# Where the even chunks of w_gate lie in SBUF: half of their rows moved 64 bytes past a multiple of 128

## The chip, the cores and the metric

The kernel runs on one core of a Trainium2 chip. The metric is device time in microseconds of one execution; the kernel before took 1170.16 us (median of three runs, 1168.32 to 1172.19). About 0.3% is what a measurement of this kernel can tell from no change.

## The reference

The program computes block-causal attention over 8 batches of 8 heads (576 positions, 64 dimensions a head) and feeds the result, as 4608 tokens of 512 features, through a gated feed-forward layer with 1536 hidden features.

```python
scores = scale * np.matmul(q, k.transpose(0, 1, 3, 2))      # masked by blocks of 64
attn = softmax(scores); x = attn @ v                        # as [4608, 512]
g = x @ w_gate                                              # [512, 1536]
silu = g * (1.0 / (1.0 + np.exp(-g)))
val = x @ w_val                                             # [512, 1536]
return (silu * val @ w_out).astype(np.float32)              # [1536, 512]
```

The three weights come as 64-bit floats, so each element is two 32-bit words for the kernel.

## The kernel before, in words

[...]

**Feed-forward tiles.** The 4608 tokens go in 18 tiles of 256. x of a tile lies in four pairs of SBUF tiles `xhl` (128 features d x 256 tokens, high and low). The 1536 hidden features go in 12 chunks of 128, and two chunks make a pair: `feed_forward` works on chunks i and i+1 together. For each pair, `up(i, 0, ...)` makes the gate (w_gate) and `up(i, 1, ...)` the value (w_val), each into one PSUM tile `gv` with the chunk i in its first 256 columns and the chunk i+1 in its second. Each chunk takes NDC = 4 rows of features d = 0..3, and three matmuls a row: 12 matmuls of 128x128 weights by 256 columns of x. So a pair is 12 matmuls with an even chunk of w_gate, 12 with an odd one, and 24 with w_val. In all there are 18 x 6 pairs, and 18 x 6 x 12 = 1296 matmuls on the even chunks. ScalarE (tanh) and VectorE then make the gated product, split it into `hhl`, and TensorE makes the down product of an earlier pair with w_out's tiles `wo`.

In tiles 0 to 3 (below FINE) each row of an up product is a task by itself, so that three matmuls can stand alone among other work. From tile 4 on, the 12 matmuls of a chunk, and the gate and value of a pair, follow each other.

**Weights in SBUF.** `weight(i, kind)` loads a chunk of a weight once, turns its 64-bit words into a float, and keeps a high part (ScalarE, L1016) and a low part (VectorE, L1019) in resident tiles. `w_at(which, x, i)` gives the place: w_val in `v_all0` and `v_all1` (x = 0 high, 1 low), the odd chunks of w_gate in `g_odd0` and `g_odd1`, the even ones in `g_even0` and `g_even1`. Each tile holds four rows d a chunk, [128 partitions, 4, columns]. Six chunks of w_out wait for a while in such places, too (AWAY), two of them in places of even chunks (c = 10 and c = 8); they are stored from there to `wo_d` in DRAM (L1038) and read there by the down products of tiles 0 and 1.

A small tile `gap` of 16 floats (64 bytes) stands between `v_all1` and `g_even0`. In the built program the tiles start at these bytes of each partition:

| tile | before | past a multiple of 128 |
|---|---|---|
| g_odd0, g_odd1 | 1,984, 14,272 | 64 |
| v_all0, v_all1 | 26,560, 51,136 | 64 |
| g_even0, g_even1 | 75,776, 88,064 | 0 |
| xhl (all), hhl, wo, parts, qk | 119,296 and on for xhl | 0 |

Every row of 128 weights has 512 bytes, and rows and chunks follow at multiples of 512 bytes, so a tile's remainder is that of each of its rows.

**Order.** `in_order` plans all tasks with a table of costs and writes out one order for each engine; nothing in it depends on addresses. Attention work of the batches (scores at L480, L607 and L691, products with v at L858) stands among the feed-forward products on TensorE until about 950 us.

Of the kernel before, what the change touches and what calls it, by code (L numbers as in the profile page):

```python
# [8 lines left out]
F32R = mybir.dt.float32r  # L9
# [9 lines left out]
def kernel(  # L19
# [17 lines left out]
    nc = tc.nc  # L37
# [3 lines left out]
    P = 128  # L41
# [5 lines left out]
    NDC = DM // P  # L47
    NFC = DFF // P
# [49 lines left out]
    const = ctx.enter_context(tc.tile_pool(name="const", bufs=1))  # L98
# [54 lines left out]
    def add(engine, cost, rank, fn, after=(), bufs=(), port=False, mode="", stage=""):  # L153


        t = Task(engine, cost, rank, fn, after, bufs, port, mode)
        for a in after:
            if a is not None:
                a.next.append(t)
                t.waits += 1  # L160
        for u in bufs:
            u.left += 1
        t.n, t.stage = len(tasks), stage
        tasks.append(t)
        return t


    def act_us(n, psum=False, more=0.0):
        return (0.05 if psum else 0.093) + n * 0.000833 + more

    def dve_us(n, one=False):
        return 0.07 + n * (0.00052 if one else 0.00104)

    def up_us(n):
        return n * 0.1134 + (0.012 if n < 3 * NDC else 0.0)
# [8 lines left out]
    def dma(rank, size, fn, after=(), bufs=(), n=1, engine="SP", packet=1024, late=0.0):  # L184

        t = add(engine, 0.5 * n, rank, fn, after, bufs)
        t.moves = size / packet * (9.5 + 0.0405 * packet) / 16e3
        t.late = 1.1 + late
        return t
# [15 lines left out]
    half_w, whole_w = [P, NDC, DFF // 2], [P, NDC, DFF]  # L205
    g_odd = [const.tile(half_w, F32R, name=f"g_odd{x}") for x in range(2)]
    v_all = [const.tile(whole_w, F32R, name=f"v_all{x}") for x in range(2)]
    const.tile([P, 16], F32, name="gap")
    g_even = [const.tile(half_w, F32R, name=f"g_even{x}") for x in range(2)]

    def w_at(which, x, i):

        if which:
            return v_all[x][:, :, i * P : (i + 1) * P]
        return (g_odd if i % 2 else g_even)[x][:, :, i // 2 * P : (i // 2 + 1) * P]

# [98 lines left out]
    for i in range(7):  # L317
        n = 2**i
# [620 lines left out]
    def words(ap):  # L939
        return ap.bitcast(I32) if wide else ap  # L940
# [11 lines left out]
    def weight(i, kind):  # L952

        R = PIECES[i][kind]
        raw = Buf("wo", "raw")
        away = AWAY.get(i) if kind == 2 else None
        wo = Buf("wo", "out") if kind == 2 and not away else None
        fs = slice(i * P, (i + 1) * P)

        parts = 1 if wo else NDC

        def part(j):
            if wo:  # L970
                return wo[0][:, j : j + 1]
            which, c = away or (kind, i)
            return w_at(which, j, c)

        def load():
            view = raw[0].rearrange("p (n m) -> p n m", n=NDC if kind < 2 else 1)
            if kind < 2:
                fs = slice(i * P * (1 + wide), (i + 1) * P * (1 + wide))
                src = words((w_gate, w_val)[kind])[:, fs].rearrange("(c p) f -> p c f", p=P)
            else:  # L980
                src = words(w_out)[i * P : (i + 1) * P, :].rearrange("p (n m) -> p n m", n=1)
            nc.sync.dma_start(out=view, in_=src)

        t = chain["w"] = dma(AHEAD.get((i, kind), R), 5e5, load, [chain["w"]], [raw], packet=1024 if kind < 2 else 4096)
        bufs = [raw, wo] if wo else [raw]

        def words_of(j):
            w = raw[0].rearrange("p (n t) -> p n t", t=1 + wide)[:, :, j]
            return w.rearrange("p (n m) -> p n m", n=parts)

        y = Buf("ob", "signs") if wide else None


        def signs():
            w = words_of(1).bitcast(F32)
            to = y[0].rearrange("p (n m) t -> p n m t", n=parts)[:, :, :, 1]
            nc.scalar.mul(to, w, 2.0**-60)  # L997

        def scaled():
            w = words_of(1).bitcast(F32)  # L1000
            nc.scalar.mul(w, w, 2.0**-112)


        def fraction():
            s = y[0].rearrange("p m t -> p (m t)").bitcast(I32).rearrange("p (n m) -> p n m", n=parts)
            nc.vector.scalar_tensor_tensor(
                words_of(0), words_of(0), 29, s, ALU.logical_shift_right, ALU.bitwise_or
            )

        def exponent():  # L1010
            nc.vector.scalar_tensor_tensor(
                words_of(0), words_of(1), 3, words_of(0), ALU.logical_shift_left, ALU.bitwise_or
            )

        def high():
            nc.scalar.copy(part(0), words_of(0).bitcast(F32))  # L1016

        def low():
            nc.vector.tensor_tensor(  # L1019
                part(1), words_of(0).bitcast(F32), part(0).bitcast(F32), ALU.subtract  # L1020
            )

        if wide:
            t = add("ACT", act_us(DM, more=0.13), R, signs, [t], [raw, y])
            f = add("DVE", dve_us(DM), R, fraction, [t], [raw, y], True)
            t = add("ACT", act_us(DM, more=0.06), R, scaled, [t], [raw])
            t = add("DVE", dve_us(DM), R, exponent, [t, f], [raw], True)
        t = w_high[i, kind] = add("ACT", act_us(DM, more=0.04), R, high, [t], bufs)
        t = add("DVE", dve_us(DM), R, low, [t], bufs, True)
        if kind == 2:  # L1030
            w_kept[i] = t, wo, part

            def store():
                if wo:
                    nc.sync.dma_start(out=wo_d[i], in_=wo[0].bitcast(F32))
                    return
                for j in range(2):
                    nc.sync.dma_start(  # L1038
                        out=wo_d[i][:, j].rearrange("p (n m) -> p n m", n=parts), in_=part(j).bitcast(F32)
                    )  # L1040

            t = dma(R, 5e5, store, [t], [wo] if wo else [], 2 if away else 1, packet=512 if away else 4096)
            if away:
                before_place.append((t, away))
        w_done[i, kind] = t
# [58 lines left out]
    def feed_forward(j, t0, w, xs):  # L1104
# [16 lines left out]
        def rank(i):  # L1121
            return (10.0 + (t0 + w * i / NFC) / S) if j > 1 else SIDE[j] + w * i / NFC / S

        def up(i, which, prev):

            ps = Buf("gv")
            ts = up_done[0]
            for y in range(2):

                for ds in [range(NDC)] if j >= FINE else [[d] for d in range(NDC)]:  # L1130

                    def products(ds=ds, y=y):
                        hi, lo = (w_at(which, k, i + y) for k in range(2))
                        o = ps[0][:, y * w : (y + 1) * w]
                        for d in ds:
                            xhi, xlo = (xs[d][1][k] for k in range(2))
                            first, last = d == 0, d == NDC - 1
                            nc.tensor.matmul(o, lhsT=hi[:, d], rhs=xhi[:, 0:w], start=first, stop=False)  # L1138
                            nc.tensor.matmul(o, lhsT=hi[:, d], rhs=xlo[:, 0:w], start=False, stop=False)  # L1139
                            nc.tensor.matmul(o, lhsT=lo[:, d], rhs=xhi[:, 0:w], start=False, stop=last)  # L1140

                    ts = add(
                        "PE",
                        up_us(3 * len(ds)),
                        rank(i),
                        products,
                        [ts, *(xs[d][0] for d in ds), w_done[i + y, which]],
                        [ps, *(xs[d][1] for d in ds)],
                        stage="up",
                    )  # L1150
                    ts.prev = prev
                    prev = ts if j >= FINE else None
            chain["up"] = up_done[0] = ts
            return ps, ts

        for i in range(0, NFC, 2):
# [11 lines left out]
            n = 2 * w  # L1168
# [29 lines left out]
            for y in range(2):  # L1198
                away = AWAY.get(i + y)
                if j == 0 or j == 1 and i + y < BOTH:  # L1200
                    wl, wo, w_part = w_kept[i + y]
                else:
                    wo, away = Buf("wo", "out"), None
# [103 lines left out]
    for i in range(NFC):  # L1307
        for kind in range(3):
            weight(i, kind)
# [173 lines left out]
```

## Time and profile before

| | |
|---|---|
| median of three runs | 1170.16 us |
| the profiled execution's own time | 1170.16 us |
| its span | 1168.3 us |
| TensorE busy (matmul) | 1154.0 us, 8788 instructions |
| VectorE, ScalarE, GpSimd busy | 743.8, 620.8, 317.2 us |
| idle time of TensorE that a wait explains, longest group | 2.2 us (a gate product behind VectorE's L1175) |

Busy time counts a matmul from its start to its modelled end, and matmuls overlap: 256 columns last some 280 ns and follow each other at less than half of that. The pace is therefore read from the distance of starts in the timeline, whose rows give start and duration in us. In the rows on stretches, the first numbers are the stretch and its length, then follow the busy time and the count of each engine, the granted clock of TensorE, the share of busy DMA and GB/s; with a tile named, they count that tile's matmuls on TensorE alone. In the rows of one line, three numbers are the shortest, median and longest duration in ns.

### The profile page before, as it was taken

The numbers are of one execution on the slowest core, as the hardware profiler recorded it, in microseconds if no ns is written. First come the engines' busy times: TensorE is split into PE (matmuls) and PEld (weight loads), VectorE is DVE, ScalarE is ACT, GpSimd is POOL, SyncE is SP. The second block draws the span as 40 slices with busy tenths as digits, with TensorE's granted clock in tenths as the row PEclk, the third lists the DMA queues.
The fourth block names the chain that finished last, engine by engine and source line by source line (L and its number), as shares of the span: only waits on it lengthen the run. The fifth ranks groups of instructions, "written<-read, shape, count | busy, mean of one in ns | idle before, by whom it ended". The sixth has DMA issues, their size and how long they took to land.

```text
span 1168.3 us, 22385 instructions
## 1 busy us (share of the span) xinstructions
PE 1154.0 (99%) x8788; PEld 1038.1 (89%) x8788; DVE 743.8 (64%) x1230; ACT 620.8 (53%) x1114; POOL 317.2 (27%) x139
## 2 busy tenths in 40 slices
PE   8999999999999999999999999999999999999998
PEld 7767888888898989899898989989898989999997
DVE  6998888768696649577474758647584753323222
ACT  6998866755665556473555638365564622212111
POOL 3122201163524422515232331524233430000000
PEclk9999999999999999999999999999999999999999
DMA  7858757675567447465647546556574335444342
GB/s 199 231 149 228 217 171 223 179 213 157 153 179 206 134 133 197 156 169 165 179 127 216 153 161 159 173 142 179 155 210 155 129 125 182 157 151 139 141 170 101
DMA packets 263786, 197.44 MB, mean 169 GB/s; under 512 B 190528, under 2 KB 228176, under 8 KB 263680
## 3 DMA queue, kind: packets, MB, share of 16 engines
q1 hardware_dynamic: 262704, 195.29, 57.5%
q8 instruction: 69, 1.13, 0.4%
q10 hardware_dynamic: 976, 0.72, 0.2%
q14 instruction: 37, 0.30, 0.1%
HBM read 171.57 MB, written 24.38 MB: 168 GB/s over the span
## 4 chain that ended last, share of the span: by engine, by line
PE 90%; ACT 5%; DVE 2%; DMA 1%; issue 0%; SPq 0%; POOL 0%; DVEq 0%; POOLq 0%; ACTq 0%
PE gv L1138 17%; PE gv L1140 16%; PE gv L1139 16%; PE at L858 8%; PE po L1230 8%; PE po L1231 7%; PE po L1232 7%; PE at L607 6%; PE at L480 1%; PE at L1230 1%; PE at L1231 1%; PE at L1232 1%; DMA wo<-in_moe_w_out_dram 1%; PE at L691 1%; ACT ob L997 1%; ACT sc L498 1%
## 5 line engine op out<-in xcount | busy, mean ns | idle before, releaser
L752 POOL PARTITION_ALL_REDUCE mx<-mx x80 | 139.8, 1799 | 414.4 <-DVE mx L748 118.2
L1138 PE MATMUL gv<-xhl,v_all 128*128 128x256 f32 x864 | 240.9, 279 | 1.4 <-DVE t L1180 1.3
L1140 PE MATMUL gv<-xhl,v_all 128*128 128x256 f32 x864 | 239.1, 277 | 0.0
L1139 PE MATMUL gv<-xhl,v_all 128*128 128x256 f32 x864 | 239.0, 277 | 0.0
L909 POOL PARTITION_ALL_REDUCE mx<-mx x48 | 174.8, 3693 | 223.7 <-DVE mx L748 186.7
L1175 DVE SCALAR_TENSOR_TENSOR t<-t,gv 128x512 f32<-128x512 f32 x108 | 74.0, 685 | 185.2 <-ACT t L1172 184.8
L1138 PEld LDWEIGHTS gv<-xhl,v_all 128*128 128x128 f32 x864 | 162.1, 188 | 3.7 <-DVE t L1180 2.0
L1139 PEld LDWEIGHTS gv<-xhl,v_all 128*128 128x128 f32 x864 | 162.2, 188 | 0.5
L1140 PEld LDWEIGHTS gv<-xhl,v_all 128*128 128x128 f32 x864 | 162.2, 188 | 0.0
L1185 ACT CAST hhl<-t 128x512 fp32r<-128x512 f32 x108 | 67.0, 621 | 174.8 <-PE po L1231 104.6
L1230 PE MATMUL po<-wo,hhl 128*128 128x512 f32 x372 | 147.7, 397 | 0.0
L1231 PE MATMUL po<-wo,hhl 128*128 128x512 f32 x372 | 145.5, 391 | 0.0
L1232 PE MATMUL po<-wo,hhl 128*128 128x512 f32 x372 | 145.1, 390 | 0.0
L1188 DVE TENSOR_TENSOR hhl<-t,hhl 128x512 fp32r<-128x512 f32 x108 | 84.2, 782 | 83.5 <-ACT hhl L1185 83.1
L1172 ACT ACTIVATE t<-gv 128x512 f32<-128x512 f32 x108 | 64.6, 598 | 129.2 <-PE gv L1140 127.2
L776 DVE TENSOR_TENSOR sc<-sc,mx 128x640 f32<-128x640 f32 (+6 forms) x168 | 121.8, 775 | 15.4 <-POOL mx L752 15.3
L1138 PE MATMUL gv<-xhl,g_even 128*128 128x256 f32 x432 | 124.1, 287 | 2.3 <-DVE t L1175 2.2
L1140 PE MATMUL gv<-xhl,g_even 128*128 128x256 f32 x432 | 122.1, 283 | 0.0
L1139 PE MATMUL gv<-xhl,g_even 128*128 128x256 f32 x432 | 122.1, 283 | 0.0
L1138 PE MATMUL gv<-xhl,g_odd 128*128 128x256 f32 x432 | 121.3, 281 | 0.0
L1140 PE MATMUL gv<-xhl,g_odd 128*128 128x256 f32 x432 | 119.4, 276 | 0.0
L1139 PE MATMUL gv<-xhl,g_odd 128*128 128x256 f32 x432 | 119.4, 276 | 0.0
(176 smaller groups left out, 2402.0 us busy)
## 6 DMA issues: line engine op xcount, KB each, us to landing
wo<-wo_d SPq DMA_DIRECT2D x200, 512.0 KB
out_dram<-ob SPq DMA_DIRECT2D x35, 256.0 KB
v<-in_v_dram SPq DMA_DIRECT2D x64, 128.0 KB
xt<-x_d SPq DMA_DIRECT2D x64, 128.0 KB
rt<-r_d SPq DMA_DIRECT2D x128, 64.0 KB
qk<-in_q_dram SPq DMA_DIRECT2D x104, 72.0 KB
qk<-in_k_dram SPq DMA_DIRECT2D x104, 72.0 KB
x_d<-xu SPq DMA_DIRECT2D x24, 288.0 KB
```

Of the source, the lines that this page charges most:

```text
L752: nc.gpsimd.partition_all_reduce(m, m, channels=P, reduce_op=bass_isa.ReduceOp.max)
L776: nc.vector.tensor_tensor(piece(c), scores_of(c), m, ALU.subtract)
L858: nc.tensor.matmul(ps[0][own(x), 1 - i if sums else i, q0 - s0 : s1 - s0], lhsT=ones if sums else vt[0][:, 2 * lane + c, own(x)], rhs=sc[0 ...
L909: nc.gpsimd.partition_all_reduce(m, m, channels=P, reduce_op=bass_isa.ReduceOp.add)
L1138: nc.tensor.matmul(o, lhsT=hi[:, d], rhs=xhi[:, 0:w], start=first, stop=False)
L1139: nc.tensor.matmul(o, lhsT=hi[:, d], rhs=xlo[:, 0:w], start=False, stop=False)
L1140: nc.tensor.matmul(o, lhsT=lo[:, d], rhs=xhi[:, 0:w], start=False, stop=last)
L1175: nc.vector.scalar_tensor_tensor(t[0][:, 0:n], t[0][:, 0:n], 1.0, pg[0][:, 0:n], ALU.add, ALU.mult)
L1188: nc.vector.tensor_tensor(hh[1][:, 0:n], t[0][:, 0:n], hh[0][:, 0:n].bitcast(F32), ALU.subtract)
L1230: nc.tensor.matmul(po, lhsT=hi, rhs=whi, start=i + y == 0, stop=False)
L1231: nc.tensor.matmul(po, lhsT=hi, rhs=wlo, start=False, stop=False)
L1232: nc.tensor.matmul(po, lhsT=lo, rhs=whi, start=False, stop=i + y == NFC - 1)
```

## The change

`g_even0` and `g_even1` become one tile `g_even` with two halves. The first half holds rows d = 0, 1 of every even chunk, high and low, the second half rows d = 2, 3. Each half is `apart` = 12 x 2 x 128 + 16 floats long, 12,352 bytes, which is 96 x 128 + 64; so the first half starts where `g_even0` did (75,776, a multiple of 128) and the second at 88,128, 64 bytes past one. `w_at` now returns a view [128, 2, 256] for an even chunk, and the new function `rows_of_w` finds row d in a view of either kind. `parts`, by which the conversion and the stores cut a chunk, becomes 2 for an even chunk instead of 4. The tile is 128 bytes longer than the two before, so all tiles behind it move up by 128 bytes (xhl from 119,296 to 119,424) and keep their remainder.

The order of instructions on every engine, their counts and their waits are the same in both programs. What differs, other than addresses, is the shape of some accesses: eight copies on ScalarE, eight subtractions on VectorE, four stores to `wo_d` and 18 down matmuls reach an even chunk's place as 2 x 256 instead of 4 x 128.

```diff
     const.tile([P, 16], F32, name="gap")
-    g_even = [const.tile(half_w, F32R, name=f"g_even{x}") for x in range(2)]
+    apart = NFC * NDC // 2 * P + 16
+    g_even = const.tile([P, 2 * apart], F32R, name="g_even")
...
         if which:
             return v_all[x][:, :, i * P : (i + 1) * P]
-        return (g_odd if i % 2 else g_even)[x][:, :, i // 2 * P : (i // 2 + 1) * P]
+        if i % 2:
+            return g_odd[x][:, :, i // 2 * P : (i // 2 + 1) * P]
+        o = (i + x) * NDC // 2 * P
+        return g_even.rearrange("p (h m) -> p h m", h=2)[:, :, o : o + NDC // 2 * P]
+
+    def rows_of_w(w, d):
+
+        n = NDC // w.shape[1]
+        return w[:, d // n, d % n * P : (d % n + 1) * P]
...
-        parts = 1 if wo else NDC
-
         def part(j):
...
+        parts = 1 if wo else part(0).shape[1]
...
-                            nc.tensor.matmul(o, lhsT=hi[:, d], rhs=xhi[:, 0:w], start=first, stop=False)
-                            nc.tensor.matmul(o, lhsT=hi[:, d], rhs=xlo[:, 0:w], start=False, stop=False)
-                            nc.tensor.matmul(o, lhsT=lo[:, d], rhs=xhi[:, 0:w], start=False, stop=last)
+                            nc.tensor.matmul(o, lhsT=rows_of_w(hi, d), rhs=xhi[:, 0:w], start=first, stop=False)
+                            nc.tensor.matmul(o, lhsT=rows_of_w(hi, d), rhs=xlo[:, 0:w], start=False, stop=False)
+                            nc.tensor.matmul(o, lhsT=rows_of_w(lo, d), rhs=xhi[:, 0:w], start=False, stop=last)
```

## The prediction

> **What bounds the kernel now.** I read the page's first two parts, then the stretches, then the timeline of TensorE.
>
> ```profile
> span 1168.3 us, 22385 instructions
> PE 1154.0 (99%) x8788; PEld 1038.1 (89%) x8788; DVE 743.8 (64%) x1230; ACT 620.8 (53%) x1114; POOL 317.2 (27%) x139
> PEclk9999999999999999999999999999999999999999
> PE 90%; ACT 5%; DVE 2%; DMA 1%; issue 0%; SPq 0%; POOL 0%; DVEq 0%; POOLq 0%; ACTq 0%
> ```
>
> TensorE is busy for 99% of the span at its full granted clock, and 90% of the chain that ended last is its work. Two stretches, all engines, tell where that holds:
>
> ```profile
> 0.00:350.00 350.00, 339.27 (x2747) 288.38 (x2748) 284.14 (x507) 251.97 (x450) 97.04 (x63) 1.00 0.69 192
> 350.00:1168.00 818.00, 814.70 (x6043) 749.76 (x6042) 459.65 (x724) 368.87 (x665) 220.20 (x76) 1.00 0.54 159
> ```
>
> After 350 us TensorE is idle for 818 - 814.70 = 3.3 us, the store at the end among it; before that for 10.7 us. So what a matmul loses or gains after 350 us shows in the end; before it, some may vanish in waits. "Busy" hides the pace, since a matmul lasts longer than the distance to the next one. One line's durations, and the same tiles in the same two stretches (g_even first, then g_odd), show that the tiles differ:
>
> ```profile
> L1140 PEld LDWEIGHTS gv<-xhl,g_even x432: 187/192/192, 28.1 to 1154.8; 128*128 128x128 f32 x144
> L1140 PE MATMUL gv<-xhl,g_even x432: 276/283/288, 28.3 to 1154.9; 128*128 128x256 f32 x144
> L1140 PEld LDWEIGHTS gv<-xhl,g_odd x432: 187/188/193, 51.6 to 1156.1; 128*128 128x128 f32 x144
> L1140 PE MATMUL gv<-xhl,g_odd x432: 276/276/285, 51.7 to 1156.2; 128*128 128x256 f32 x144
> ...
> 0.00:350.00 350.00, 49.87 (x318) 1.00 0.69 192
> 350.00:1168.00 818.00, 133.23 (x998) 1.00 0.54 159
> ...
> 0.00:350.00 350.00, 46.66 (x306) 1.00 0.69 192
> 350.00:1168.00 818.00, 127.95 (x1008) 1.00 0.54 159
> ```
>
> After 350 us an even matmul costs 133.23/998 = 133.5 ns of TensorE, an odd one 127.95/1008 = 126.9 ns, each with a share of a tail: 6.6 ns more, with the same x, shape and PSUM tiles. In the built program g_even begins at a multiple of 128 bytes; g_odd, and v_all with it, lie 64 bytes past one. The timeline gives the paces themselves (start, duration):
>
> ```profile
> 403.49 0.39 PE L1232 MATMUL po<-wo,hhl 128*128 128x512 f32 x1
> 403.71 0.28 PE L1138 MATMUL gv<-xhl,g_even 128*128 128x256 f32 x1
> 404.43 0.28 PE L1138 MATMUL gv<-xhl,g_even 128*128 128x256 f32 x1
> 405.15 0.28 PE L1138 MATMUL gv<-xhl,g_odd 128*128 128x256 f32 x1
> 406.51 0.28 PE L1138 MATMUL gv<-xhl,v_all 128*128 128x256 f32 x1
> 409.23 0.28 PE L1138 MATMUL gv<-xhl,g_even 128*128 128x256 f32 x1
> ```
>
> Twelve even matmuls take 405.15 - 403.71 = 1.44 us, 120 ns each, and each half of the chunk 0.72 us. Twelve odd ones take 1.36 us, 113.3 ns each; the 24 of w_val take 2.72 us, 113.3 ns each. But the place alone doesn't set the pace. Earlier in the program:
>
> ```profile
> 274.15 0.39 PE L1232 MATMUL po<-wo,hhl 128*128 128x512 f32 x1
> 274.37 0.28 PE L1138 MATMUL gv<-xhl,v_all 128*128 128x256 f32 x1
> 277.20 0.28 PE L1138 MATMUL gv<-xhl,g_even 128*128 128x256 f32 x1
> 277.91 0.28 PE L1138 MATMUL gv<-xhl,g_even 128*128 128x256 f32 x1
> 278.63 0.28 PE L1138 MATMUL gv<-xhl,g_odd 128*128 128x256 f32 x1
> 279.87 0.28 PE L1140 MATMUL gv<-xhl,g_odd 128*128 128x256 f32 x1
> ```
>
> Here the 24 of v_all, at the same place, come right behind a down product and take 277.20 - 274.37 = 2.83 us, 117.9 ns each. Then a slow even chunk passes, and the odd one behind it runs at (279.87 - 278.63)/11 = 112.7 ns. So there are **three paces**: slow (120) for weights at a multiple of 128, and for weights 64 past one either middle (118) or quick (113.3). Which of the two seems to be set on entry: behind a down product it is middle, behind a slow even chunk quick. The even chunk is not only a loss; it also seems to put what follows into step.
>
> **The change, part by part.** Rows d = 0, 1 of each even chunk (6 matmuls, high and low parts) stay at a multiple of 128, rows d = 2, 3 (the next 6) go 64 bytes past one. Order, counts and waits are as before, on every engine; no queue is passed.
>
> 1. *Chunks that have settled by their sixth matmul.* By start stamps, 83 whole even chunks start after 350 us. In 80 of them the spacing is 0.12 us from the fourth matmul on at the latest. The first and the last are:
>
> ```profile
> 375.59 0.28 PE L1138 MATMUL gv<-xhl,g_even 128*128 128x256 f32 x1
> 377.03 0.28 PE L1138 MATMUL gv<-xhl,g_odd 128*128 128x256 f32 x1
> ...
> 1153.56 0.28 PE L1138 MATMUL gv<-xhl,g_even 128*128 128x256 f32 x1
> 1154.99 0.28 PE L1138 MATMUL gv<-xhl,g_odd 128*128 128x256 f32 x1
> ```
>
> There I let rows 2 and 3 do what the odd chunk does now behind the slow one: 113.3 instead of 120, 6 x 6.7 = 40 ns a chunk, 80 x 40 = **3.2 us** less. What comes behind stays quick. Nothing beside TensorE limits this: ScalarE waits for it, not the other way round:
>
> ```profile
> ACT t L1172 <- PE gv L1140: 127.2, 64, 5.0
> ```
>
> 2. *The three others after 350 us, and the 318 - 2 = 316 even matmuls (26 chunks' worth) before it.* Three of the early chunks have settled as above: 0.1 us less. The rest come in at the middle pace or in pieces of three to nine, like the one at 277.20, whose first six take 277.91 - 277.20 = 0.71 us and which is in step only behind them. If six slow matmuls don't do there, rows 2 and 3 run at 118 instead of 120, a gain of 12 ns a chunk, but up to 36 matmuls behind them run at 118 instead of 113.3, a loss of up to 36 x 4.6 = 166 ns. Bounds: if six do, some 26 x 15 ns = 0.4 us less, and 0.1 us less for the three; if not, 0.3 us less for rows 2 and 3, 3 x 0.15 = 0.45 us more for the three, and for the 11 whole early chunks that reach 120 only near their seventh matmul up to 11 x 0.1 = 1.1 us more (the quick runs behind them are 3 to 36 long). That is from -0.5 to +1.2 us; I take the middle, **+0.4 us**, since the early row shows step only past the sixth.
>
> 3. *Copies, stores, other readers.* Eight casts and eight subtractions write two runs of 256 instead of four of 128, all before 180 us. Four runs and one run bracket two:
>
> ```profile
> L1016 ACT CAST g_even<-wo x8: 648/670/705, 14.3 to 179.2; 128x512 fp32r<-128x512 f32 x8
> L1016 ACT CAST wo<-wo x6: 652/674/680, 127.3 to 204.9; 128x512 fp32r<-128x512 f32 x6
> ```
>
> That is 4 ns each, 16 x 4 = 0.06 us at most either way, beside other work: nothing. Four stores out of g_even move rows of 1 KB instead of 512 bytes, on SP among hundreds, while DMA is 1% of the chain; nothing, between 0 and the 0.1 us of a few shorter transfers. Eighteen down matmuls read g_even as moving operand in two runs instead of four: nothing.
>
> The sum: -3.2 + 0.4 = -2.8 us. The profiled execution took 1170.16 us for its span of 1168.3; it is also the median of the three runs (1168.32 to 1172.19). So **1167.4 us**.
>
> [...]
>
> **Rivals.**
>
> *The place isn't the cause: 1170 us.* The even chunk is also the first of each pair, behind a down product; if this made it slow, moving half of it changes nothing. For it: in the late pairs, order and place can't be told apart. Against it: at 277.20 and at 409.23 an even chunk comes behind v_all and is slow too, and v_all behind a down product runs at 118, not 120.
>
> *Six slow matmuls don't set the step: slower, 1183 us.* Place: the boundary between the sixth and seventh matmul of each even chunk. If what follows falls to the middle pace, rows 2 and 3 gain 12 ns, but the 36 matmuls of the odd chunk and of w_val lose 36 x 4.6 = 166 ns: 154 ns for each of 83 pairs, 12.8 us. It decides from the point where fewer than 154/(154 + 40) = 79% of the late chunks settle in time: there gain and loss cancel. For it: the early row with 0.71 us. Against it: the late rows, where the slow pace stands within the first three or four.
>
> *All chunks settle: 1165.8 us.* Rows 2 and 3 of all 108 chunks become quick: 108 x 40 ns = 4.3 us. Against it: the early 118.
>
> *The shift counts.* x and all tiles behind g_even move up by 128 bytes, but v_all and g_odd do not. If distance counted in steps of 256 bytes, their 3888 matmuls could turn slow: 3888 x 6.7 ns = 26 us, 1196 us. No row tells 128 from 256 for them.
>
> **How the numbers follow.** My forecast has 0.60, no effect 0.14, all settle 0.13, six are too few 0.10, the shift 0.03. About 0.3% (3.5 us) is what a measurement can tell from no change. The forecast, 2.8 us, lies inside it by 0.7 us, and the three runs spread over 3.9 us, so I give it 0.38 for faster by more and 0.62 for within: faster 0.60 x 0.38 + 0.13 x 0.85 = 0.34; slower 0.13 and a little for drift, 0.14; same the rest, 0.52. The range from 1164 (all settle, with 1.8 us of spread) to 1173 (no effect, with 2 or 3 us) leaves out the two slower cases.
>
> **What would show it.** In the timeline of the changed kernel, late even chunks take 6 x 120 + 6 x 113.3 = 1.40 us instead of 1.44, and the odd one behind still 1.36. The row of L1140's successor on g_even gets two kinds of durations, 283 and 276. After 350 us the even tile's cost per matmul falls from 133.5 to about 130.2 ns. Wrong would be: an odd chunk of 1.41 us (out of step), a late even chunk still of 1.44 us (place not the cause), or v_all at 120.

## The result: 1.2% slower

The changed kernel took 1184.13 us (median of four runs, 1182.61 to 1185.28) against 1169.93 us (four runs, 1168.32 to 1172.19) for the kernel before: a ratio of 1.0119 [1.0099, 1.014], 14 us more, outside the range of the forecast and on the other side.

The page of the changed kernel, first two parts and the shares of the chain:

```profile
span 1182.5 us, 22385 instructions
PE 1168.0 (99%) x8788; PEld 1051.9 (89%) x8788; DVE 744.6 (63%) x1230; ACT 620.7 (52%) x1114; POOL 316.2 (27%) x139
PEclk9999999999999999999999999999999999999999
PE 90%; ACT 5%; DVE 2%; DMA 2%; SPq 1%; issue 0%; POOL 0%; DVEq 0%; POOLq 0%; ACTq 0%
```

The count of matmuls and the clock are as before. The span is 14.2 us longer, and TensorE is busy 14.0 us more (1168.0 against 1154.0). No new wait is needed to account for it. The stretches of the changed kernel say where: all engines first (PE, PEld, DVE, ACT, POOL), then the matmuls of g_even, g_odd and v_all alone after 350 us.

```profile
0.00:350.00 350.00, 339.08 (x2738) 287.97 (x2739) 282.39 (x505) 250.68 (x449) 97.10 (x63) 1.00 0.69 191
350.00:1182.00 832.00, 828.88 (x6053) 763.89 (x6051) 462.17 (x726) 370.04 (x666) 219.14 (x76) 1.00 0.53 157
...
350.00:1182.00 832.00, 134.24 (x1008) 1.00 0.53 157
...
350.00:1182.00 832.00, 132.28 (x1008) 1.00 0.53 157
...
350.00:1182.00 832.00, 252.44 (x2025) 1.00 0.53 157
```

In the first 350 us TensorE is busy for as long as before (339.08 us against 339.27) but runs 9 matmuls fewer (2738 against 2747), about 1.1 us of work at 0.12 us each. Whether that belongs to the change is open: e5 and e12 below, which are one and the same kernel, differ by 18 matmuls there (2749 and 2731). Behind 350 us TensorE is still idle for only 832 - 828.88 = 3.1 us. The tile that was changed costs 134.24/1008 = 133.2 ns a matmul, against 133.5 before. Most of the loss sits in two tiles that were not moved. g_odd costs 131.2 ns instead of 126.9, which is 132.28 - 127.95 = 4.33 us over the same 1008 matmuls. v_all stood before at

```profile
350.00:1168.00 818.00, 243.77 (x2025) 1.00 0.54 159
```

so it gives 252.44 - 243.77 = 8.67 us over the same 2025. Together that is 13.0 of the 14.2 us; the 9 matmuls that slipped behind 350 us are about the rest.

The timeline of TensorE shows a late pair of the changed kernel (start, duration), whose rows L1147 to L1149 answer to L1138 to L1140 before (w high by x high, w high by x low, w low by x high):

```profile
405.20 0.29 PE L1147 MATMUL gv<-xhl,g_even 128*128 128x256 f32 x1
405.93 0.28 PE L1147 MATMUL gv<-xhl,g_even 128*128 128x256 f32 x1
406.64 0.28 PE L1147 MATMUL gv<-xhl,g_odd 128*128 128x256 f32 x1
408.06 0.28 PE L1147 MATMUL gv<-xhl,v_all 128*128 128x256 f32 x1
410.88 0.28 PE L1147 MATMUL gv<-xhl,g_even 128*128 128x256 f32 x1
```

Rows 0 and 1 take 0.73 us, slow as before. Rows 2 and 3 take 406.64 - 405.93 = 0.71 us, 118 ns each: not the quick pace but the middle one. The odd chunk, which took 1.36 us, takes 1.42 us (118 ns each), and the 24 of w_val take 2.82 us instead of 2.72. So the kernel has all but lost its quick pace. Counted over all whole odd chunks that start after 350 us, by the distance of starts: before, 83 of 84 have a mean below 116.7 ns a matmul; after, 2 of 84. This count is given for each experiment below as "odd chunks at the quick pace".

### The profile page after: what moved, and what is told of

It reads as the page before. It is cut to its first block, busy times and chain, and to the rows that moved or that the text cites. A ratio compares the mean times of both kernels' runs of the same rounds, so it can differ in the third digit from the quotient of the medians.

```text
span 1182.5 us, 22385 instructions
## 1 busy us (share of the span) xinstructions
PE 1168.0 (99%) x8788; PEld 1051.9 (89%) x8788; DVE 744.6 (63%) x1230; ACT 620.7 (52%) x1114; POOL 316.2 (27%) x139
## 4 chain that ended last, share of the span: by engine, by line
PE 90%; ACT 5%; DVE 2%; DMA 2%; SPq 1%; issue 0%; POOL 0%; DVEq 0%; POOLq 0%; ACTq 0%
PE gv L1147 17%; PE gv L1148 16%; PE gv L1149 16%; PE at L867 8%; PE po L1239 8%; PE po L1241 7%; PE po L1240 7%; PE at L616 6%; PE at L489 1%; PE at L1239 1%; PE at L1241 1%; PE at L1240 1%; ACT ob L1006 1%; ACT sc L507 1%; ACT sc L789 1%; ACT wo L1010 1%
## 5 line engine op out<-in xcount | busy, mean ns | idle before, releaser
L1147 PE MATMUL gv<-xhl,v_all 128*128 128x256 f32 x864 | 244.3, 283 | 1.2 <-DVE t L1189 1.2
L1149 PE MATMUL gv<-xhl,v_all 128*128 128x256 f32 x864 | 242.6, 281 | 0.0
L1148 PE MATMUL gv<-xhl,v_all 128*128 128x256 f32 x864 | 242.4, 281 | 0.0
L1184 DVE SCALAR_TENSOR_TENSOR t<-t,gv 128x512 f32<-128x512 f32 x108 | 73.9, 684 | 190.3 <-ACT t L1181 189.7
L1147 PEld LDWEIGHTS gv<-xhl,v_all 128*128 128x128 f32 x864 | 165.2, 191 | 3.5 <-DVE t L1189 1.6
L1149 PEld LDWEIGHTS gv<-xhl,v_all 128*128 128x128 f32 x864 | 162.3, 188 | 0.0
L1147 PE MATMUL gv<-xhl,g_even 128*128 128x256 f32 x432 | 124.4, 288 | 2.4 <-DVE t L1184 2.4
L1147 PE MATMUL gv<-xhl,g_odd 128*128 128x256 f32 x432 | 123.0, 285 | 0.0
L1189 DVE SCALAR_TENSOR_TENSOR t<-t,gv 128x512 f32<-128x512 f32 x108 | 73.9, 684 | 77.1 <-PE gv L1149 76.1
L1149 PE MATMUL gv<-xhl,g_even 128*128 128x256 f32 x432 | 122.0, 282 | 0.0
L1148 PE MATMUL gv<-xhl,g_odd 128*128 128x256 f32 x432 | 121.3, 281 | 0.0
```

What stands on the lines that cost most here:

```text
L1147: nc.tensor.matmul(o, lhsT=rows_of_w(hi, d), rhs=xhi[:, 0:w], start=first, stop=False)
L1148: nc.tensor.matmul(o, lhsT=rows_of_w(hi, d), rhs=xlo[:, 0:w], start=False, stop=False)
L1149: nc.tensor.matmul(o, lhsT=rows_of_w(lo, d), rhs=xhi[:, 0:w], start=False, stop=last)
L1184: nc.vector.scalar_tensor_tensor(t[0][:, 0:n], t[0][:, 0:n], 1.0, pg[0][:, 0:n], ALU.add, ALU.mult)
```

## The experiments

What was open after the result: are six slow matmuls too few, does the shift of x by 128 bytes do it, does the new layout as such, or does the *place* of the second half matter in a way that a remainder of 128 doesn't show? Modulo 256 the places are finer than in the table of tiles ahead of the prediction. The numbers under x, even and odd are bytes past a multiple of 256:

| kernel | x | even, rows 0 and 1 | even, rows 2 and 3 | odd and w_val | time, ratio to before | odd chunks at the quick pace |
|---|---|---|---|---|---|---|
| before | 0 | 0 | 0 | 192 | 1 | 83 of 84 |
| after | 128 | 0 | 64 | 192 | 1.0119 | 2 of 84 |
| e1 | 128 | 0 | 0 | 192 | 0.9995 | 84 of 84 |
| e2 | 0 | 0 | 64 | 192 | 1.0099 | 0 of 84 |
| e3 | 0 | 192 | 192 | 192 | 1.0067 | 2 of 84 |
| e5, e12 | 0 | 0 | 192 | 192 | 0.998, 0.9981 | 79 of 83, 79 of 84 |
| e6 | 0 | 0 | 0 | 192 | 1.0004 | 83 of 84 |
| e7 | 0 | 192 | 0 | 192 | 1.0094 | 12 of 84 |
| e8 | 0 | 0 | 0 | 64 | 1.0104 | 1 of 84 |
| e11 | 0 | 128 | 128 | 64 | 1.0011 | 83 of 83 |

All ratios are to the kernel before on the same chip, as the record gives them with their intervals; they need not equal the quotient of the two medians (for e2 that is 1185.6/1171.11 = 1.0124). The weights of a down product, `hhl`, lie at 0 in all of these but the change and e1, where they move with x to 128; e4, e9 and e10 move them by themselves.

### e1: the shift alone

To the kernel before only 128 bytes are added behind g_even, so that x and what follows move as in the change:

```diff
     g_even = [const.tile(half_w, F32R, name=f"g_even{x}") for x in range(2)]
+    const.tile([P, 32], F32, name="pad")
```

> The kernel before with 128 unused bytes behind g_even: every tile behind it (x among them) moves up by 128 bytes as in the change, and the even chunks stay whole at a multiple of 128. Theory S (six slow matmuls don't bring what follows into step, the shift is idle): nothing changes, 1170 us, odd and w_val chunks at 113.3 ns a matmul. Theory H (the shift of x against weights that stayed counts, in steps of 256 bytes): the odd and w_val chunks run at some 118 ns as in the change, 36 x 4.6 ns x 83 pairs = 13.7 us more, about 1184 us.

Measured: 1171.57 us, ratio 0.9995 [0.998, 1.001]. The stretch and the late pair of e1, v_all alone and then the timeline:

```profile
350.00:1171.00 821.00, 244.10 (x2028) 1.00 0.53 159
```

```profile
405.50 0.29 PE L1139 MATMUL gv<-xhl,g_even 128*128 128x256 f32 x1
406.95 0.28 PE L1139 MATMUL gv<-xhl,g_odd 128*128 128x256 f32 x1
408.31 0.28 PE L1139 MATMUL gv<-xhl,v_all 128*128 128x256 f32 x1
```

v_all costs 244.10/2028 = 120.4 ns a matmul, as before, and the odd chunk takes 1.36 us. The shift of x by 128 bytes costs nothing that can be measured.

### e2: the halves without the shift

To the changed kernel the same pad is added, which brings x back to a multiple of 256:

```diff
     g_even = const.tile([P, 2 * apart], F32R, name="g_even")
+    const.tile([P, 32], F32, name="pad")
```

> The change with 128 more unused bytes behind g_even, so that x and all that follows it stands 256 bytes from where it stood before, the same place modulo 256. Theory S: as the change, 1184 us. Theory H: the odd and w_val chunks are quick again, and rows 2 and 3 of the even chunks with them: 1167 us (the forecast's 2.8 us less than before).

Measured: 1185.6 us, ratio 1.0099 [1.0065, 1.0133]; v_all at 252.70/2028 = 124.6 ns, as in the changed kernel. The loss comes with the halves (1.0099), not with the shift (e1, 0.9995). The late pair of e2:

```profile
407.63 0.28 PE L1148 MATMUL gv<-xhl,g_even 128*128 128x256 f32 x1
408.34 0.28 PE L1148 MATMUL gv<-xhl,g_even 128*128 128x256 f32 x1
409.05 0.28 PE L1148 MATMUL gv<-xhl,g_odd 128*128 128x256 f32 x1
410.47 0.28 PE L1148 MATMUL gv<-xhl,v_all 128*128 128x256 f32 x1
```

Within the first six the last three starts lie 120 ns apart, which by the forecast's own measure was settled; the next six still take 0.71 us.

### e3: all weights 64 bytes past a multiple of 128

The gap is moved behind g_even, so that the even chunks lie at 192 like the others, and x stays:

```diff
-    const.tile([P, 16], F32, name="gap")
     g_even = [const.tile(half_w, F32R, name=f"g_even{x}") for x in range(2)]
+    const.tile([P, 16], F32, name="gap")
```

> The kernel before with the gap of 64 bytes moved behind g_even: all weights of the up products lie 64 bytes past a multiple of 128, x where it was. If a slow even chunk is needed to bring the rest into step (part of theory S): all 48 matmuls of a late pair at 118 ns, 48 x 117.9 - (12 x 120 + 36 x 113.3) = 140 ns a pair more, 83 pairs, 11.6 us, about 1182 us. If the pace is set by place alone (theory H in its plain form): all 48 at 113.3, 80 ns a pair less, 6.7 us, about 1163 us.

Measured: 1181.07 us, ratio 1.0067 [1.004, 1.0094]. The stretches of e3 after 350 us, g_even and then v_all:

```profile
350.00:1179.00 829.00, 132.58 (x1008) 1.00 0.53 157
...
350.00:1179.00 829.00, 251.98 (x2025) 1.00 0.53 157
```

The even chunks gain 133.5 - 131.5 = 2.0 ns a matmul by their place alone. But v_all loses 251.98 - 243.77 = 8.2 us: with no slow stretch, 82 of 84 odd chunks run at the middle pace. The quick pace behind the slow even chunk (83 of 84 before) is all but gone without it (2 of 84 here), as the forecast supposed.

### e4: the down products' weights 64 bytes past

In the kernel before, `hhl` is moved to 64 and what follows back:

```diff
+        if tag == "hhl":
+            const.tile([P, 16], F32, name="pad0")
...
+    const.tile([P, 48], F32, name="pad1")
```

> The kernel before with 64 unused bytes ahead of hhl and 192 behind it, so that the stationary operand of the down products lies 64 bytes past a multiple of 128 and the moving one at a multiple, as in the quick up products; all else keeps its place modulo 256. If the pace of any matmul hangs on the place of weights against the moving operand: down matmuls fall from 227 to about 220 ns, 1296 x 7 = 9 us less, 1161 us, unless what follows them falls out of step (up to 14 us more, 1175 us). If the rule holds for up products only: 1170 us.

Measured: 1176.22 us, ratio 1.0034 [1.0018, 1.005]. The matmuls on hhl after 350 us, in e4 and then in the kernel before:

```profile
350.00:1175.00 825.00, 255.00 (x1029) 1.00 0.53 159
```

```profile
350.00:1168.00 818.00, 248.91 (x1020) 1.00 0.54 159
```

That is 247.8 against 244.0 ns for a down matmul: 3.8 ns, some 4 us over a thousand of them. The odd chunks stay quick (84 of 84). So these 512-column matmuls gained nothing from weights 64 bytes past a multiple of 128.

### e5: the second half at 192 instead of 64

After these four, the place modulo 256 was the suspect. In e5 the second half of the change goes 192 bytes past instead of 64, and x stays at a multiple of 256:

```diff
-    apart = NFC * NDC // 2 * P + 16
-    g_even = const.tile([P, 2 * apart], F32R, name="g_even")
+    apart = NFC * NDC // 2 * P + 48
+    g_even = const.tile([P, 2 * apart - 32], F32R, name="g_even")
```

(The view of two halves is then built with its distance written out, since the tile is shorter than two of them.)

> The change with its second half 192 bytes instead of 64 past a multiple of 256, and 64 unused bytes behind, so that x and all behind it stand 256 bytes from before. Rows 2 and 3 then lie against x exactly as the odd and w_val chunks do (192 past a multiple of 256), rows 0 and 1 at a multiple, as before. If the residue modulo 256 decides whether the seventh matmul goes over to the quick pace (theory R): 1167 us, late even chunks of 1.40 us, odd ones of 1.36. If six slow matmuls are too few, or the step is only found at a chunk's border (theory S): 1184 us, odd chunks of 1.41 us.

Measured: 1168.84 us, ratio 0.998 [0.9967, 0.9992]. The stretch of e5, g_even and then v_all, and its late pair:

```profile
350.00:1165.00 815.00, 129.88 (x997) 1.00 0.54 160
...
350.00:1165.00 815.00, 244.26 (x2025) 1.00 0.54 160
```

```profile
403.48 0.28 PE L1150 MATMUL gv<-xhl,g_even 128*128 128x256 f32 x1
404.19 0.28 PE L1150 MATMUL gv<-xhl,g_even 128*128 128x256 f32 x1
404.87 0.28 PE L1150 MATMUL gv<-xhl,g_odd 128*128 128x256 f32 x1
406.23 0.28 PE L1150 MATMUL gv<-xhl,v_all 128*128 128x256 f32 x1
408.95 0.28 PE L1150 MATMUL gv<-xhl,g_even 128*128 128x256 f32 x1
```

Here rows 2 and 3 do what the forecast said of the change: 404.87 - 404.19 = 0.68 us, 113.3 ns each, and the odd chunk and w_val stay at 1.36 and 2.72 us. An even matmul costs 129.88/997 = 130.3 ns. Between e2 and e5 the second half's place modulo 256 differs, 64 against 192, and nothing else that the matmuls read; it makes 1.2% by their ratios (1.0099 and 0.998), some 14 us, or 17 us by their medians on two chips (1185.6 against 1168.84). Six slow matmuls are enough here: 79 of 83 odd chunks are quick.

### e6: the new layout with no offset

```diff
-    apart = NFC * NDC // 2 * P + 16
+    apart = NFC * NDC // 2 * P
```

> The change without its 16 extra floats: halves as in the change (rows 512 bytes apart, low beside high, two runs in copies and stores), but both at a multiple of 128, and x where it stood before. If the new layout as such, not the 64 bytes, breaks the step (theory L): about 1184 us. Theories S and R: the even chunk is slow throughout, what follows is quick, 1170 us.

Measured: 1171.54 us, ratio 1.0004 [0.9991, 1.0017]; v_all 243.76 us over 2025, g_even 133.18 over 998, within 0.1 us of before. The two halves and the wider accesses alone change nothing.

### e7: the halves the other way round

Rows 0 and 1 at 192, rows 2 and 3 at a multiple of 256, x and the rest as in the kernel before:

```diff
-    const.tile([P, 16], F32, name="gap")
     apart = NFC * NDC // 2 * P + 16
     g_even = const.tile([P, 2 * apart], F32R, name="g_even")
+    const.tile([P, 48], F32, name="pad")
```

> The change with the halves' places swapped: no gap ahead of g_even, so rows 0 and 1 lie 192 bytes past a multiple of 256, like the odd chunks, and rows 2 and 3 at a multiple; x stands 256 bytes from before. Now the six slow matmuls come last in the even chunk, at its border to the odd one. If six slow ones at that border suffice: rows 0 and 1 enter behind a down product at 118, rows 2 and 3 at 120, the rest quick: 12 ns a pair less than before, 1169 us. If six are too few anywhere (theory S): 1183 us.

Measured: 1182.6 us, ratio 1.0094 [1.007, 1.0117]. Two pairs of e7 that follow each other; the second comes directly behind w_val:

```profile
404.54 0.28 PE L1147 MATMUL gv<-xhl,g_even 128*128 128x256 f32 x1
405.25 0.28 PE L1147 MATMUL gv<-xhl,g_even 128*128 128x256 f32 x1
405.96 0.28 PE L1147 MATMUL gv<-xhl,g_odd 128*128 128x256 f32 x1
407.37 0.28 PE L1147 MATMUL gv<-xhl,v_all 128*128 128x256 f32 x1
410.20 0.28 PE L1147 MATMUL gv<-xhl,g_even 128*128 128x256 f32 x1
...
411.62 0.28 PE L1147 MATMUL gv<-xhl,g_odd 128*128 128x256 f32 x1
412.98 0.28 PE L1147 MATMUL gv<-xhl,v_all 128*128 128x256 f32 x1
```

In the first pair rows 0 and 1 run at the middle pace, and rows 2 and 3 pass in 0.71 us without reaching 120 ns; the odd chunk stays at the middle pace (1.41 us). In the second pair the odd chunk takes 412.98 - 411.62 = 1.36 us, the quick pace. That happens in 12 of 84. By the instruction just ahead of the even chunk, the starts in e7's timeline split so: behind w_val all 8 odd chunks are quick, behind a down product 1 of 58. So six slow matmuls are not always enough: in 72 of 84 pairs of e7 they were not, and the count differs by what stands ahead of the chunk. How that acts, these runs don't tell.

### e8: a full slow chunk, and the odd one at 64

This keeps all twelve slow matmuls and moves the odd chunks and w_val to 64 instead of 192:

```diff
+    const.tile([P, 32], F32, name="pad")
     g_odd = [const.tile(half_w, F32R, name=f"g_odd{x}") for x in range(2)]
...
-    const.tile([P, 16], F32, name="gap")
+    const.tile([P, 48], F32, name="gap")
```

> The kernel before with 128 unused bytes ahead of g_odd and a gap of 192 instead of 64 bytes: the even chunks (all 12 matmuls slow) and x at a multiple of 256 as before, but the odd and w_val chunks 64 instead of 192 bytes past one. Theory R (weights at 64 past a multiple of 256 don't become quick behind slow ones, those at 192 do): odd and w_val chunks at 118, 36 x 4.6 ns x 83 pairs = 13.7 us more, 1185 us. If the residue modulo 128 is what counts and six slow matmuls were too few (theory S): twelve slow ones precede here, so quick, 1171 us.

Measured: 1183.32 us, ratio 1.0104 [1.0077, 1.0131]. Stretch of v_all, and the late pair of e8:

```profile
350.00:1181.00 831.00, 252.55 (x2025) 1.00 0.52 157
```

```profile
404.79 0.28 PE L1139 MATMUL gv<-xhl,g_even 128*128 128x256 f32 x1
406.21 0.28 PE L1139 MATMUL gv<-xhl,g_odd 128*128 128x256 f32 x1
407.63 0.28 PE L1139 MATMUL gv<-xhl,v_all 128*128 128x256 f32 x1
```

The odd chunk behind twelve slow matmuls takes 1.42 us, and v_all costs 252.55 us, as after the change. (The even chunk takes 1.42 us here instead of 1.44; from its second matmul to the last the starts lie 119 or 120 ns apart, as before.) So a slow stretch of full length doesn't help weights at 64 (1 of 84 odd chunks quick). With e5, where half a stretch is enough (79 of 83), this rules out that the change was slower because its slow stretch was cut in half.

### e9 and e10: the down products' weights at 192

e9 is the kernel before with `hhl` at 192; e10 is e5 with `hhl` at 192.

```diff
+        if tag == "hhl":
+            const.tile([P, 48], F32, name="pad0")
...
+    const.tile([P, 16], F32, name="pad1")
```

In e10 `hhl` is laid out ahead of the other buffers:

```diff
-    g_even = const.tile([P, 2 * apart - 32], F32R, name="g_even")
+    g_even = const.tile([P, 2 * apart - 48], F32R, name="g_even")
...
-    first_of = [("v", ""), ("ob", "signs" if wide else "out"), ("parts", "pair"), ("xhl", ""), ("wo", "raw"), ("hhl", "")]
+    first_of = [("hhl", ""), ("v", ""), ("ob", "signs" if wide else "out"), ("parts", "pair"), ("xhl", ""), ("wo", "raw")]
...
+        if tag == "hhl":
+            const.tile([P, 16], F32, name="pad")
```

> The kernel before with hhl, the stationary operand of the down products, 192 bytes past a multiple of 256 (192 unused bytes ahead of it, 64 behind), all else in its place modulo 256. If the quick pace reaches over from w_val to the down products (both 192 past): down matmuls fall from 229 to about 220 ns, 1296 x 9 = 11.7 us less, 1159 us. If a down matmul of 512 columns doesn't follow this rule, as with 64 past in the earlier run: 233 ns, 4 ns x 1296 = 5 us more, 1176 us.

> The halves with the second 192 bytes past a multiple of 256 (1169 us in the earlier run) and hhl 192 past one too, laid ahead of the other buffers. If both effects hold and add up: 1169 - 11.7 = 1157 us. If hhl at 192 past makes the down products slower: 1174 us. If the entry from a quick down product spoils the step of the even chunk: odd and w_val chunks at 118 again, 14 us more than either.

Measured: e9 1178.56 us, ratio 1.0058 [1.0038, 1.0079]; e10 1178.82 us, ratio 1.0058 [1.0038, 1.0078]. The down products are no faster: e9's matmuls on hhl after 350 us are

```profile
350.00:1176.00 826.00, 249.48 (x1020) 1.00 0.53 158
```

against 248.91 us for the same count before. What gets worse is the up products: v_all costs 248.79 us in e9 and 249.46 in e10 (2025 each), and only 33 of 83 odd chunks in e9, and 27 of 83 in e10, are at the quick pace. In e9 a pair whose even chunk takes a full 1.44 us (403.25 to 404.69) can still be followed by an odd chunk of 1.42 us (404.69 to 406.11):

```profile
403.25 0.28 PE L1141 MATMUL gv<-xhl,g_even 128*128 128x256 f32 x1
404.69 0.28 PE L1141 MATMUL gv<-xhl,g_odd 128*128 128x256 f32 x1
406.11 0.28 PE L1141 MATMUL gv<-xhl,v_all 128*128 128x256 f32 x1
```

It goes by what stands ahead: of the 58 late pairs of e9 whose even chunk starts right behind a down product 50 have an odd chunk at the middle pace, of the 25 other pairs none. So the odd chunks 192 bytes past the slow ones were quick in this kernel with its down weights at 0 (before, 83 of 84), 64 (e4, 84 of 84) and 128 (e1, 84 of 84) past a multiple of 256; with these at 192, 50 of 83 (e9) and 56 of 83 (e10) were not. Why, these runs don't tell.

### e11: the distance or the absolute place

The even chunks at 128, the odd ones and w_val at 64, which again is 192 past the even ones modulo 256:

```diff
+    const.tile([P, 32], F32, name="pad0")
     g_odd = [const.tile(half_w, F32R, name=f"g_odd{x}") for x in range(2)]
...
     g_even = [const.tile(half_w, F32R, name=f"g_even{x}") for x in range(2)]
+    const.tile([P, 32], F32, name="pad1")
```

> The kernel before with 128 unused bytes ahead of g_odd and 128 behind g_even: the even chunks lie 128, the odd and w_val chunks 64 bytes past a multiple of 256, x at one. The odd ones are 192 bytes behind the place of the even ones, as before, but no longer 192 past a multiple of 256. If the distance from the slow weights decides (theory D): quick behind slow, 1171 us. If the place itself modulo 256 decides (theory R): odd and w_val chunks at 118, 1184 us.

Measured: 1171.49 us, ratio 1.0011 [1.0, 1.0023]. Stretch of v_all, and the late pair of e11:

```profile
350.00:1168.00 818.00, 243.57 (x2025) 1.00 0.53 159
```

```profile
402.47 0.29 PE L1140 MATMUL gv<-xhl,g_even 128*128 128x256 f32 x1
403.92 0.28 PE L1140 MATMUL gv<-xhl,g_odd 128*128 128x256 f32 x1
405.28 0.28 PE L1140 MATMUL gv<-xhl,v_all 128*128 128x256 f32 x1
```

With the odd chunks at 64, where e8 was 12 us slower, they now run at 1.36 us, and v_all is as before. So in these kernels the pace goes with the distance from the slow weights' place (192 modulo 256: 1.36 us here; 64: 1.42 us in e8), not with the place itself. It goes with the distance modulo 256, not modulo 512: the quick step is 448 bytes modulo 512 before and here (83 of 84 and 83 of 83 odd chunks), and 192 in e5 (79 of 83), while the step that stays at the middle pace is 64 in e2 (0 of 84 quick) and 320 in e8 (1 of 84). Nor is it the distance from x: odd chunks 64 past x are quick in e1 (84 of 84) and e11 (83 of 83) and middle in e8 (1 of 84 quick).

### e12: e5 again, timed more closely

> The halves with the second 192 bytes past a multiple of 256 once more, in more rounds, since its gain is near what can be told: 0.998 of the kernel before in the earlier run, 2.2 us. By the late chunks, 12 x 120 to 6 x 119 + 6 x 113.6, 83 pairs x 40 ns = 3.3 us at most; from 1 to 3.5 us less expected.

Measured: 1168.49 us (eleven runs) against 1170.32 us (twenty), ratio 0.9981 [0.9969, 0.9992]. With e5 that is twice a gain of about 2 us; it is the fastest version here, and ahead of both kernels, though by less than the 0.3% that a single comparison can tell.

## Why the prediction was wrong

**What bounds the kernel, and the three paces: right.** TensorE's pace after 350 us is the time: it is idle there for 3.1 us of 832, and over the whole span the busy times of VectorE, ScalarE and GpSimd moved by at most 1.0 us (GpSimd, 317.2 to 316.2). Taken over six matmuls or more, the changed kernel shows the slow pace (0.73 us for six) and the middle one (0.71 us for six, 1.42 us for twelve) again, and the quick one in 2 of 84 odd chunks (single distances of its slow rows mostly lie between 117 and 124 ns); e3 shows both supposed roles of the slow chunk: away from its place it costs 131.5 ns a matmul instead of 133.5, and without it 2 of 84 odd chunks are quick.

**The step that failed: item 1 of the sum**, that rows 2 and 3 "do what the odd chunk does now behind the slow one". It put them 64 bytes past a multiple of 128 and took that for the odd chunk's place. By the remainder of 128 they are the same; modulo 256 the odd chunk lies 192 bytes past the even one, and rows 2 and 3 lie 64 past. The forecast said of x that "no row tells 128 from 256", and gave it 0.03; the same doubt, asked of the second half itself, was left out. The places in the built program were known to the byte, so the question could have been seen without a run, though not its answer. What the runs showed in place of the term of -3.2 us: rows 2 and 3 at 118 ns (a gain of 0.3 us over 1008 even matmuls, 133.5 to 133.2 ns), and 13.0 us lost on the odd chunks and w_val.

**The size of the term held where the place was right.** In e5 an even matmul costs 130.3 ns, where the forecast had about 130.2; 79 of 83 odd chunks are quick, where it had counted on 80 settled pairs of 83; and the gain is 2.2 us (e5) and 1.8 us (e12), where the sum had 2.8.

**Item 2, the early stretch: not told apart from noise.** By 350 us the changed kernel is 9 matmuls behind, about 1.1 us where +0.4 was forecast with a bound of +1.2; but e5 and e12, the same kernel, lie 18 matmuls apart there.

**Item 3, copies and stores: nothing, as said.** e6, which has all of them, is at 1.0004. The 0.1 us that bounded the four stores was an estimate of the author's that no row gives; their issues on SP took 367/457/460 ns before (L1038; shortest, median, longest) and 367/438/461 after (L1047).

**The rivals.** *Six slow matmuls don't set the step* had the right place, mechanism of loss and price: 1183 us against 1184.13, 12.8 us against 13.0 in the two tiles. Its cause was another: e8, with twelve settled slow matmuls, loses as much (1.0104), and e5, with six, gains. It isn't wholly false, since in e7 six behind rows at the middle pace were too few in 57 of the 58 pairs behind a down product. *The shift counts* had the step of 256 bytes, but of the wrong tile: e1 is at 0.9995. *The place isn't the cause* falls with e3, e8 and e5, whose orders are the same (1.0067, 1.0104 and 0.998); e2 and e5 have x at the same byte, too, differ in the place of weights alone, and lie at 1.0099 and 0.998. Where the step stayed at 192 modulo 256, moving weights did change nothing (e11, 1.0011). *All chunks settle* needs the quick pace and falls with it; in e5, four of 83 late odd chunks stay at the middle pace.

**What stays open.** Whether fewer than six slow matmuls would do, a step of 128 bytes out of the slow rows, and e5 with x 128 bytes further, were not tried. Why the pace goes by 256 bytes is not shown by any run. Nor is it shown whether "slow" (120 ns) means a multiple of 128 as such or the remainder of x, since x lay at a multiple of 128 in every kernel. In e7 and e9 the pace differs by what stands ahead of a pair (e7: 8 of 8 quick behind w_val, 1 of 58 behind a down product; e9: 8 of 58 behind a down product, 25 of 25 behind all else), and e10 has 27 of 83 quick where e5 has 79; no run gives the cause.

## What to carry to other kernels

When a matmul-bound kernel's pace differs between tiles of one shape, read the distance of starts by tile and lay it beside the byte addresses of the weights, modulo 256 and not only modulo 128: with the same two halves, pad bytes alone moved this kernel between 1168.5 us (e12) and 1185.6 us (e2). Here the group behind the slow one was quick in 83 of 84 pairs, and in 2 of 84 once the slow one was gone (e3), so judge an edit to a slow group by what follows it, not by its own time. Where an edit rests on "the same place as a tile that does well", move it by that tile's own remainder, and time the other remainders beside it.

## What the runs showed of the hardware that was not expected

- Weights of 128x256 float32r matmuls that came behind slow matmuls (weights at a multiple of 128 bytes, 120 ns) ran at 113.3 ns when they lay 192 bytes past those weights modulo 256 (before, e1, e5, e6, e11, e12: 79 to 84 of 83 or 84 late odd chunks), and at 118 ns when the step out of the slow stretch was 64 (after, e2, e8: 0 to 2). Both have the same remainder of 128. This held with the down products' weights at 0, 64 or 128 modulo 256; at 192 (e9, e10) only 33 and 27 of 83 were quick.
- The middle pace mostly lasted once it was there: in the changed kernel through the rest of the even chunk (0.71 us for six), the odd chunk (1.42 us) and the 24 of w_val (2.82 us), 117.5 to 118.3 ns each, with 2 of 84 odd chunks quick. With all weights at one place (e3), 82 of 84 late odd chunks were at it.
- The down products, of 512 columns, did not go the same way: with their weights at 64 they cost 3.8 ns more (e4, 247.8 against 244.0), with their weights at 192 nothing less (e9, 249.48 us against 248.91 for 1020), and in that kernel v_all cost 248.79 us where it had cost 243.77.
